# Key-value products of a linear attention: head pairs on 64-lane halves, or single heads on 64x64 quarters of the array

## The chip, the cores and the metric

The kernel runs on one core of a Trainium2 chip. The metric is the device time of one execution in microseconds (us), the median of several runs. A hardware profile of one execution is shown beside it: PE is TensorE's matmuls, PEld its weight loads, DVE is VectorE, ACT is ScalarE, POOL is GpSimd and SP is SyncE, whose queue issues most DMAs. L295 is line 295 of the kernel file.

## What is computed

Inputs are q, k and v of shape 8 batches x 8 heads x 576 positions x 64 (f32), and two weight matrices, 512 x 2048 and 2048 x 512 (f32). The output is 4608 x 512 in f32.

```python
def _attn_ref(q, k, v):
    q_s = np.exp(q - np.max(q, axis=-1, keepdims=True))
    q_s = q_s / (np.sum(q_s, axis=-1, keepdims=True) + 1e-09)
    k_s = np.exp(k - np.max(k, axis=2, keepdims=True))
    k_s = k_s / (np.sum(k_s, axis=2, keepdims=True) + 1e-09)
    kv = np.einsum('bhsd,bhse->bhde', k_s, v)
    return np.einsum('bhsd,bhde->bhse', q_s, kv)

x = attn_out.transpose(0, 2, 1, 3).reshape(8 * 576, 8 * 64)
h = x @ w_in
out = np.maximum(0.01 * h, h) @ w_out
```

The part that matters here is `kv`: for each batch and head, a 64 x 64 matrix, summed over 576 positions, of exponentiated k against v. The division by the sum over positions is done on the result: the sum of each k column comes out of the same product if v has a further column of ones.

## The kernel before

**Layout.** One batch of q, k or v lies in SBUF as 128 partitions x 4 x 9 x 64. Eight heads are spread so: partitions 0 to 63 hold the first head of each of four pairs and partitions 64 to 127 the second (index `hh` is 0 or 1), 64 partitions are 64 groups of positions, and r runs over the 9 positions of a group. In the program's names, head 2 x hl + hh has its rows in half hh and its place hl among four; hl is written as 2 x gg + hp.

**Attention of one batch.** k's maximum over positions (DVE, and for batch 0 PE), the subtraction (POOL or DVE), the exponential into `ke` in bf16 (ACT, L203), a cast of v into `vb` in bf16 (`v_cast`, ACT or POOL). q goes through its own maximum, exponential, sum and normalisation into `qe`, and is transposed (by PE for batches 0 and 1, by DMA for the others). Then three steps follow on the array:

1. `kv` (batches 1 to 7, L295) or `kv_pair` (batch 0, in two halves, L371): the key-value products. The stationary operand is `ke` of one row half (64 partitions) and of two heads (hp 0 and 1), 64 x 128; the moving operand is `vb` of the same 64 partitions, 129 columns: 64 of one head, 64 of the other and one column of ones. The result, 128 x 129 in PSUM, has the two wanted 64 x 64 products on its diagonal, two unwanted ones beside them, and the sums in column 128. Nine matmuls (r) accumulate into one result. The two row halves alternate in program order and write to two PSUM banks. One batch takes 2 x 9 x 2 = 36 matmuls.
2. `kd_make` (L310, L313), for batch 0 `kd_rec` and `kd_one` (L382, L387): DVE takes the reciprocal of the sums and writes the diagonal blocks, scaled, into `kd`, whose other blocks are zero. `kd_one` does it with one instruction over 128 x 128 and a mask `block` of ones on the diagonal blocks.
3. `attend` (L418) or `attend_x` (L446): `kd`, 128 x 128, times the transposed q, 256 to 320 columns at a time, and a copy to `xT` by ACT or DVE.

**Two dense layers.** The 4608 rows of x are taken in 9 tiles of 512. For each, `layer1` (L458) makes 16 blocks of hidden units by 4 matmuls each of 512 columns, `leaky` (L467, ACT) writes them to `gj` in bf16, and `layer2` (L479) adds 16 matmuls for each of 4 groups of 128 rows; the result is copied (L473, mostly DVE) and stored. The first tile is worked in two halves of 256 columns.

**Order.** The schedule is written out by hand. `at(t, u, ...)` hangs attention steps of a batch onto step u of dense tile t, and `run(t, u)` calls them there, so on PE's queue a batch's key-value stage stands between two matmuls of the dense layers, some 4 us or more before the first `attend` of that batch. PE works its queue in order. Batch 0 has no dense work ahead of it: its stages run in the first 20 us, padded by `wake`, matmuls on zeros (L324), while the weights of the layers are still being loaded by POOL's queue (L133).

The PSUM results `pkv` come from a pool of six one-bank buffers which the layers share.

Of the kernel before, what the change touches and what calls it, by code (L numbers as in the profile page):

```python
# [8 lines left out]
FP32 = mybir.dt.float32  # L9
BF16 = mybir.dt.bfloat16  # L10
AF = mybir.ActivationFunctionType
ALU = mybir.AluOpType
# [7 lines left out]
L = 64  # L20
R = 9
# [4 lines left out]
def kernel(  # L26
# [9 lines left out]
    nc = tc.nc  # L36
# [3 lines left out]
    B, H, S, D = q.shape  # L40
# [6 lines left out]
    P = 128  # L47
# [7 lines left out]
    const_pool = ctx.enter_context(tc.tile_pool(name="const", bufs=1))  # L55
# [11 lines left out]
    psB_pool = ctx.enter_context(tc.tile_pool(name="psB", bufs=6, space=bass.MemoryType.PSUM))  # L67
    psO_pool = ctx.enter_context(tc.tile_pool(name="psO", bufs=2, space=bass.MemoryType.PSUM))
    BANK_TAG = "bank2k"


    def load(src, b, name, cuts):
# [15 lines left out]
    st = [{} for _ in range(B)]  # L88
# [7 lines left out]
        out=st[0]["q"][:, :, RB].rearrange("p h r d -> p h (r d)"),  # L96
        in_=qflat[:, :, RB].rearrange("p h r d -> p h (r d)"),
# [8 lines left out]
    block = const_pool.tile([P, P], FP32)  # L106
# [9 lines left out]
    xT = xT_pool.tile([P, NB, T], BF16)  # L116


    vb2 = [const_pool.tile([P, R, 2, 130], BF16, name=f"vb{i}") for i in range(2)]
    kd2 = [const_pool.tile([P, NB, P], BF16, name=f"kd{i}") for i in range(2)]  # L120
    for i in range(2):
        nc.gpsimd.memset(vb2[i][:, :, :, 128:129], 1.0)
        nc.gpsimd.memset(kd2[i], 0.0)


# [81 lines left out]
        )  # L207

    def v_cast(eng, b, gg):
        o = vb2[b % 2][:, :, gg, 0:128].rearrange("p r (h d) -> p h r d", h=2)  # L210
        i = st[b]["v"][:, 2 * gg : 2 * gg + 2]
        if eng is nc.scalar:
            eng.copy(out=o, in_=i)
        else:
            eng.tensor_copy(out=o, in_=i)  # L215
# [69 lines left out]
        )  # L285


    def kv(b):

        pkv = [psB_pool.tile([P, 2, 130], FP32, name="pkv", tag=BANK_TAG) for _ in range(2)]  # L290
        for gg in range(2):
            for r in range(R):
                for hh in range(2):
                    rows = slice(hh * L, (hh + 1) * L)
                    nc.tensor.matmul(  # L295
                        pkv[hh][:, gg, 0:129],
                        lhsT=st[b]["ke"][rows, r, 2 * gg : 2 * gg + 2].rearrange(
                            "p h d -> p (h d)"
                        ),
                        rhs=vb2[b % 2][rows, r, gg, 0:129],  # L300
                        start=(r == 0),
                        stop=(r == R - 1),
                    )
        st[b]["pkv"] = pkv

    def kd_make(b):
        for hh in range(2):
            pkv = st[b]["pkv"][hh]
            krec = small_pool.tile([P, 2, 1], FP32, name="krec")
            nc.vector.reciprocal(out=krec, in_=pkv[:, :, 128:129])  # L310
            for hp in range(2):
                p0 = hp * D
                nc.vector.tensor_tensor(  # L313
                    out=kd2[b % 2][p0 : p0 + D, 2 * hh : 2 * hh + 2, p0 : p0 + D],
                    in0=pkv[p0 : p0 + D, :, p0 : p0 + D],
                    in1=krec[p0 : p0 + D].to_broadcast([D, 2, D]),
                    op=ALU.mult,
                )
# [45 lines left out]
        )  # L364

    def kv_pair(b, gg):
        pkv = [psB_pool.tile([P, 130], FP32, name="pkv1", tag=BANK_TAG) for _ in range(2)]
        for r in range(R):
            for hh in range(2):
                rows = slice(hh * L, (hh + 1) * L)  # L370
                nc.tensor.matmul(  # L371
                    pkv[hh][:, 0:129],
                    lhsT=st[b]["ke"][rows, r, 2 * gg : 2 * gg + 2].rearrange("p h d -> p (h d)"),
                    rhs=vb2[b % 2][rows, r, gg, 0:129],
                    start=(r == 0),
                    stop=(r == R - 1),
                )
        st[b]["pkv", gg] = pkv

    def kd_rec(b, gg, hh):  # L380
        st[b]["krec", gg, hh] = krec = small_pool.tile([P, 1], FP32, name="krec1")
        nc.vector.reciprocal(out=krec, in_=st[b]["pkv", gg][hh][:, 128:129])  # L382

    def kd_one(eng, b, gg, hh):
        pkv, krec = st[b]["pkv", gg][hh], st[b]["krec", gg, hh]
        o = kd2[b % 2][:, 2 * hh + gg]
        eng.scalar_tensor_tensor(  # L387
            out=o, in0=pkv[:, 0:P], scalar=krec, in1=block, op0=ALU.mult, op1=ALU.mult
        )

    def q_transpose(b, r0, n):
# [145 lines left out]
    k_sub_ps(0, 0, HB)  # L537
    k_exp(0, slice(1, 2))
    v_cast(nc.scalar, 0, 0)
    v_cast(nc.scalar, 0, 1)  # L540
    k_sub_ps(0, 1)
    nc.gpsimd.tensor_copy(out=gate[:, 0:1], in_=st[0]["k"][:, HL - 1, R - 1, D - 1 : D])  # L542
    load_w_in(1)
    k_exp(0, H1)
    q_first_rec(0, RA)
    q_norm(0, RA)
    kv_pair(0, 0)
    wake(4)
    q_transpose(0, 0, 4)
    kv_pair(0, 1)  # L550
    for hh in range(2):
        kd_rec(0, 0, hh)
        kd_one(nc.vector, 0, 0, hh)
    q_keep(nc.scalar, 0, 0, 4, slice(0, 4, 2))
    q_keep(nc.vector, 0, 0, 4, slice(1, 4, 2))
    attend(0, [0, 2], 0, 256, nc.scalar)
    wake(3)
    kd_rec(0, 1, 0)
    kd_rec(0, 1, 1)
    kd_one(nc.vector, 0, 1, 0)  # L560
    kd_one(nc.vector, 0, 1, 1)
    q_max(0, R1)
    q_sub(nc.gpsimd, 0, R1)
# [25 lines left out]
    at(0, 15, lambda: q_max(1, RB), lambda: q_sub(nc.gpsimd, 1, RB))  # L589
    at(0, 29, lambda: k_exp(1, H1))  # L590
    at(0, 31, lambda: v_cast(nc.scalar, 1, 0), lambda: k_exp(1, H0))
    at(0, 33, lambda: q_exp(1, RA), lambda: q_sum(1, RA), lambda: q_norm(1, RA))
    at(0, 33, lambda: v_cast(nc.scalar, 1, 1), lambda: q_exp(1, RB), lambda: q_sum(1, RB))
    at(0, 41, lambda: kv(1))
    at(0, 41, lambda: q_norm(1, RB), lambda: kd_make(1))
    for r0 in (0, 2):
        at(0, 41, lambda r0=r0: q_transpose(1, r0, 2), lambda r0=r0: q_keep(nc.scalar, 1, r0, 2))
# [10 lines left out]
    def plan(b, o):  # L608
        t = b - 2
        at(t, o, lambda: k_begin(b), lambda: q_begin(b), lambda: k_tree(b, ALLH))  # L610
        at(t, o + 3, lambda: k_allmax(b), lambda: k_sub(nc.gpsimd, b, ALLH))
        at(t, o + 7, lambda: q_max(b, ALLR), lambda: q_sub(nc.gpsimd, b, ALLR))
        at(t, o + 11, lambda: k_exp(b, ALLH))
        at(t, o + 12, lambda: v_cast(nc.gpsimd, b, 0), lambda: v_cast(nc.gpsimd, b, 1))
        at(t, o + 16, lambda: q_exp(b, ALLR))
        at(t, o + 18, lambda: q_sum(b, ALLR))
        at(t, o + 21, lambda: q_norm(b, ALLR))
        kvu, pu = o + (24 if b == 3 else 25), o + (33 if b == 3 else 34)
        at(t, kvu, lambda: kv(b))
        at(t, kvu + 1, lambda: kd_make(b))  # L620
        at(t, o + 22, lambda: q_turn(b))
        for i in range(8):
            at(t, pu + i // 2, lambda i=i: attend_x(b, i // 2, XR[i % 2], nc.scalar))


    def plan2():
        b = 2
        at(1, 0, lambda: k_begin(b), lambda: q_begin(b), lambda: k_tree(b, ALLH))
        at(1, 3, lambda: k_allmax(b))
        at(1, 6, lambda: k_sub(nc.vector, b, H0), lambda: k_sub(nc.vector, b, H1))  # L630
        at(1, 9, lambda: k_exp(b, ALLH))
        for rs in XR:
            at(1, 9, lambda rs=rs: q_max(b, rs), lambda rs=rs: q_sub(nc.gpsimd, b, rs))
        at(1, 13, lambda: v_cast(nc.gpsimd, b, 0), lambda: v_cast(nc.gpsimd, b, 1))
        for i, rs in enumerate(XR):
            at(1, (13, 16)[i], lambda rs=rs: q_exp(b, rs), lambda rs=rs: q_sum(b, rs), lambda rs=rs: q_norm(b, rs))
            at(1, (15, 17)[i], lambda rs=rs: q_turn(b, rs))
        at(1, 23, lambda: kv(b))
        at(1, 24, lambda: kd_make(b))
        for i in range(8):  # L640
            at(1, 28 + i // 2, lambda i=i: attend_x(b, GS[i % 4], XR[i // 4], nc.scalar))
# [91 lines left out]
```

## Time and profile before

| | us |
|---|---|
| median of 3 runs | 293.1 (292.87 to 293.29) |
| the profiled execution, whole | 293.27 |
| its span, first to last instruction | 291.5 |
| TensorE busy (of the span) | 280.2 (96%) |
| ScalarE busy | 149.7 (51%) |
| VectorE busy | 147.0 (50%) |
| GpSimd busy | 85.5 (29%) |
| granted TensorE clock, mean | 1.000 |

Busy time of PE is the union of its matmuls' records; a matmul's record is its latency, and records of neighbouring matmuls overlap, so a group's busy time is less than its count times its mean. The chain that ended last is the sequence of work, followed back from the last instruction, in which each piece was released by the one before it. Times in a timeline or chain are counted from the start of the span.

### The profile page before, as it was taken

How to read it: one execution, taken by the hardware profiler on the slowest of the kernel's cores; microseconds unless marked ns; L12 is line 12 of the kernel's file. 1: busy time of each engine (PE TensorE's matmuls, PEld its weight loads, DVE VectorE, ACT ScalarE, POOL GpSimd, SP SyncE). 2: the span in 40 equal slices, each digit the busy share in tenths (PEclk: the TensorE clock that was granted, in tenths of full speed). 3: DMA queues.
4: the chain of work that ended last, by engine and by line, in shares of the span. 5: the costliest groups of instructions: out<-in, count | busy, mean ns of one | idle time of the engine just before them, and what ended most of it. 6: DMA issues, size and time to landing. Idle time of an engine off the chain costs nothing.

```text
span 291.5 us, 4277 instructions
## 1 busy us (share of the span) xinstructions
PE 280.2 (96%) x1645; PEld 139.9 (48%) x1672; DVE 147.0 (50%) x244; ACT 149.7 (51%) x268; POOL 85.5 (29%) x61
## 2 busy tenths in 40 slices
PE   8697999999999999999999999999999999999995
PEld 3265845444544544454444544554455444444443
DVE  2947957896790796289276546645541200110011
ACT  4957683568168506941684339533953066017400
POOL 4545280008039208703910391029200000000000
PEclk9999999999999999999999999999999999999999
DMA  7999999597639454973299139913141310131032
GB/s 255 314 202 378 256 176 397 139 286 270 124 89 338 162 119 108 336 211 86 65 338 250 36 72 318 287 36 74 36 81 38 72 36 1 38 75 33 0 73 73
DMA packets 36580, 45.76 MB, mean 157 GB/s; under 512 B 15952, under 2 KB 19280, under 8 KB 36560
## 3 DMA queue, kind: packets, MB, share of 16 engines
q1 hardware_dynamic: 33120, 41.16, 48.4%
q0 software_dynamic: 3280, 4.20, 8.3%
q8 instruction: 13, 0.21, 0.3%
q10 hardware_dynamic: 160, 0.13, 0.1%
q14 instruction: 7, 0.06, 0.1%
HBM read 36.70 MB, written 9.44 MB: 158 GB/s over the span
## 4 chain that ended last, share of the span: by engine, by line
PE 89%; DMA 3%; DVE 1%; issue 1%; ACT 1%; POOL 1%; ACTq 0%
PE pout L479 43%; PE ph L458 41%; DMA w_in_sb<-in_moe_w_in_dram 3%; PE pkv L295 3%; PE po L446 2%; DVE k_raw L362 1%; PE psum_qt L395 1%; POOL w_in_sb L133 0%; ACT gj L467 0%; ACT xT L428 0%; PE po L418 0%; DVE out_sb L473 0%; POOL gate L542 0%; ACTq L467 0%
## 5 line engine op out<-in xcount | busy, mean ns | idle before, releaser
L479 PE MATMUL pout<-w_out_sb,gj 128*128 128x512 bf16 (+2 forms) x580 | 129.6, 373 | 0.6
L458 PE MATMUL ph<-xT,w_in_sb 128*128 128x512 bf16 (+1 forms) x626 | 126.8, 357 | 3.4 <-ACT xT L428 1.4
L467 ACT ACTIVATE gj<-ph 128x512 bf16<-128x512 f32 x144 | 82.5, 603 | 58.1 <-PE ph L458 57.5
L458 PEld LDWEIGHTS <-w_in_sb 128*128 128x128 bf16 x640 | 62.1, 98 | 64.8 <-issue 4.1
L479 PEld LDWEIGHTS <-gj 128*128 128x128 bf16 x592 | 57.0, 98 | 62.1 <-ACT gj L467 0.4
L473 DVE COPY out_sb<-pout 128x512 f32<-128x512 f32 (+1 forms) x34 | 22.7, 675 | 86.2 <-PE pout L479 80.7
L195 POOL TENSOR_TENSOR k_raw<-k_raw,kall 128x2304 f32<-128x2304 f32 (+1 forms) x6 | 29.1, 4846 | 83.5 <-DVE kall L187 56.3
L273 DVE TENSOR_REDUCE qsum<-qe 128x36 f32<-128x2304 bf16 (+4 forms) x11 | 19.8, 1799 | 37.4 <-ACT qe L264 37.4
L256 POOL TENSOR_TENSOR q_raw<-q_raw,qmax 128x2304 f32<-128x2304 f32 (+4 forms) x11 | 31.1, 2839 | 25.4 <-DVE qmax L226 25.4
L452 ACT CAST xT<-po 128x320 bf16<-128x320 f32 (+1 forms) x48 | 16.8, 402 | 41.2 <-PE po L446 41.2
L203 ACT ACTIVATE ke<-k_raw 128x2304 bf16<-128x2304 f32 (+2 forms) x11 | 17.6, 1596 | 10.3 <-POOL k_raw L195 8.6
L280 DVE TENSOR_TENSOR qe<-qe,qrec 128x2304 bf16<-128x2304 bf16 (+4 forms) x12 | 21.7, 1811 | 0.4
L226 DVE TENSOR_REDUCE qmax<-q_raw 128x36 f32<-128x2304 f32 (+4 forms) x11 | 19.4, 1789 | 0.0
L264 ACT ACTIVATE qe<-q_raw 128x2304 bf16<-128x2304 f32 (+4 forms) x11 | 16.9, 1533 | 0.8 <-POOL q_raw L256 0.8
L215 POOL CAST vb<-v_raw 128x1152 bf16<-128x1152 f32 x12 | 13.5, 1153 | 0.0
L324 PE MATMUL pout<-zero 128*128 128x512 bf16 x29 | 9.6, 470 | 1.5 <-POOL zero L101 1.3
L162 DVE TENSOR_TENSOR t<-k_raw 128x1024 f32<-128x1024 f32 (+1 forms) x10 | 10.1, 1011 | 0.5 <-DMA k_raw<-in_k_dram 0.2
L162 DVE TENSOR_TENSOR t<-t 128x256 f32<-128x256 f32 (+2 forms) x20 | 9.6, 478 | 0.7
L446 PE MATMUL po<-qX,kd 128*128 128x320 bf16 (+1 forms) x48 | 9.8, 286 | 0.0
L473 ACT COPY out_sb<-pout 128x512 f32<-128x512 f32 (+1 forms) x3 | 1.7, 563 | 14.9 <-PE pout L479 14.9
L295 PEld LDWEIGHTS <-ke 64*128 64x128 bf16 x252 | 7.2, 93 | 3.0 <-ACT gj L467 1.7
L313 DVE TENSOR_TENSOR kd<-pkv,krec 64x128 bf16<-64x128 f32 x28 | 8.1, 289 | 0.7
(57 smaller groups left out, 104.8 us busy)
## 6 DMA issues: line engine op xcount, KB each, us to landing
out_dram<-out_sb SPq DMA_DIRECT2D x70, 128.0 KB, 2.4
q_raw<-in_q_dram SPq DMA_DIRECT2D x7, 1152.0 KB, 8.4
v_raw<-in_v_dram SPq DMA_DIRECT2D x7, 1152.0 KB, 11.4
k_raw<-in_k_dram SPq DMA_DIRECT2D x6, 1152.0 KB, 6.1
k_raw<-in_k_dram SPq DMA_DIRECT2D x4, 576.0 KB, 5.7
w_in_sb<-in_moe_w_in_dram POOLq DMA_DIRECT2D x8, 256.0 KB, 6.7
w_out_sb<-in_moe_w_out_dram POOLq DMA_DIRECT2D x3, 512.0 KB, 13.2
v_raw<-in_v_dram SPq DMA_DIRECT2D x2, 576.0 KB, 7.7
```

The lines of the kernel that those rows point to most:

```text
L162: nc.vector.tensor_tensor(out=o, in0=i0, in1=i1, op=ALU.max)
L195: eng.tensor_tensor(out=ks, in0=ks, in1=st[b]["kall"][:, hs].unsqueeze(2).to_broadcast([P, n, R, D]), op=ALU.subtract,)
L203: nc.scalar.activation(out=st[b]["ke"][:, :, hs].rearrange("p r h d -> p h r d"), in_=st[b]["k"][:, hs], func=AF.Exp,)
L226: nc.vector.tensor_reduce(out=m, in_=st[b]["q"][:, :, rs], axis=AX.X, op=ALU.max)
L256: eng.tensor_tensor(out=qs, in0=qs, in1=st[b]["qmax", rs.start].unsqueeze(3).to_broadcast([P, HL, n, D]), op=ALU.subtract,)
L264: nc.scalar.activation(out=st[b]["qe"][:, rs].rearrange("p r h d -> p h r d"), in_=st[b]["q"][:, :, rs], func=AF.Exp,)
L273: nc.vector.reduce_sum(out=qsum, in_=st[b]["qe"][:, rs], axis=AX.X)
L280: nc.vector.tensor_tensor(out=qes, in0=qes, in1=st[b]["qrec", rs.start].unsqueeze(3).to_broadcast([P, n, HL, D]), op=ALU.mult,)
L458: nc.tensor.matmul(ph, lhsT=w_in_sb[:, cb, j * P : (j + 1) * P], rhs=xT[:, cb, c0 : c0 + n], start=(i == 0 and first), stop=(i == NB - 1 a ...
L467: nc.scalar.activation(out=o, in_=ph, func=AF.Prelu, alpha=LEAKY_SLOPE)
L473: copy(out=out_sb, in_=pout)
L479: nc.tensor.matmul(pout, lhsT=g_sb[j // 2][:, j % 2, tsub * P : (tsub + 1) * P], rhs=w_out_sb[:, j, os], start=(j == 0), stop=(j == NF - 1),)
```

## The change

The products are made for each head alone. The stationary operand is 64 x 64 (one head, one row half), the moving operand 65 columns (that head's v and a column of ones of its own), and the result goes to partitions 0 to 63 or 64 to 127 of the same PSUM buffer by the head's place hp. Four matmuls, one for each (hp, hh), now stand where two stood, 72 per batch. `vb` holds two blocks of 66 columns for each pair in place of one of 130, and the reciprocal and the kd steps read columns 0 to 63 and 64 of the narrower result. In `kd_one` the 64 columns are read twice by a broadcast, and the mask keeps the diagonal blocks.

```diff
-    vb2 = [const_pool.tile([P, R, 2, 130], BF16, name=f"vb{i}") for i in range(2)]
+    vb2 = [const_pool.tile([P, R, 2, 2, D + 2], BF16, name=f"vb{i}") for i in range(2)]
...
-        nc.gpsimd.memset(vb2[i][:, :, :, 128:129], 1.0)
+        nc.gpsimd.memset(vb2[i][:, :, :, :, D : D + 1], 1.0)
...
-        o = vb2[b % 2][:, :, gg, 0:128].rearrange("p r (h d) -> p h r d", h=2)
+        o = vb2[b % 2][:, :, gg, :, 0:D].rearrange("p r h d -> p h r d")
...
-    def kv(b):
-
-        pkv = [psB_pool.tile([P, 2, 130], FP32, name="pkv", tag=BANK_TAG) for _ in range(2)]
-        for gg in range(2):
-            for r in range(R):
+    def kv_quads(b, gg, outs):
+        for r in range(R):
+            for hp in range(2):
                 for hh in range(2):
                     rows = slice(hh * L, (hh + 1) * L)
                     nc.tensor.matmul(
-                        pkv[hh][:, gg, 0:129],
-                        lhsT=st[b]["ke"][rows, r, 2 * gg : 2 * gg + 2].rearrange(
-                            "p h d -> p (h d)"
-                        ),
-                        rhs=vb2[b % 2][rows, r, gg, 0:129],
+                        outs[hh][hp * D : (hp + 1) * D, 0 : D + 1],
+                        lhsT=st[b]["ke"][rows, r, 2 * gg + hp],
+                        rhs=vb2[b % 2][rows, r, gg, hp, 0 : D + 1],
                         start=(r == 0),
                         stop=(r == R - 1),
                     )
+
+    def kv(b):
+
+        pkv = [psB_pool.tile([P, 2, D + 2], FP32, name="pkv", tag=BANK_TAG) for _ in range(2)]
+        for gg in range(2):
+            kv_quads(b, gg, [pkv[hh][:, gg] for hh in range(2)])
...
-            nc.vector.reciprocal(out=krec, in_=pkv[:, :, 128:129])
+            nc.vector.reciprocal(out=krec, in_=pkv[:, :, D : D + 1])
...
-                    in0=pkv[p0 : p0 + D, :, p0 : p0 + D],
+                    in0=pkv[p0 : p0 + D, :, 0:D],
...
     def kv_pair(b, gg):
-        pkv = [psB_pool.tile([P, 130], FP32, name="pkv1", tag=BANK_TAG) for _ in range(2)]
...
+        pkv = [psB_pool.tile([P, D + 2], FP32, name="pkv1", tag=BANK_TAG) for _ in range(2)]
+        kv_quads(b, gg, pkv)
...
-        nc.vector.reciprocal(out=krec, in_=st[b]["pkv", gg][hh][:, 128:129])
+        nc.vector.reciprocal(out=krec, in_=st[b]["pkv", gg][hh][:, D : D + 1])
...
-            out=o, in0=pkv[:, 0:P], scalar=krec, in1=block, op0=ALU.mult, op1=ALU.mult
+            out=kd2[b % 2][:, 2 * hh + gg].rearrange("p (h d) -> p h d", h=2),
+            in0=pkv[:, 0:D].unsqueeze(1).to_broadcast([P, 2, D]),
+            scalar=krec,
+            in1=block.rearrange("p (h d) -> p h d", h=2),
+            op0=ALU.mult,
+            op1=ALU.mult,
```

More of the change, by code (lines that the diff above doesn't have):

```diff
@@ L366, in kv_pair @@
     def kv_pair(b, gg):
-        pkv = [psB_pool.tile([P, 130], FP32, name="pkv1", tag=BANK_TAG) for _ in range(2)]
[L368 to L377, printed above, removed]
+        pkv = [psB_pool.tile([P, D + 2], FP32, name="pkv1", tag=BANK_TAG) for _ in range(2)]
+        kv_quads(b, gg, pkv)
         st[b]["pkv", gg] = pkv
@@ L381, in kd_rec @@
         st[b]["krec", gg, hh] = krec = small_pool.tile([P, 1], FP32, name="krec1")
-        nc.vector.reciprocal(out=krec, in_=st[b]["pkv", gg][hh][:, 128:129])
+        nc.vector.reciprocal(out=krec, in_=st[b]["pkv", gg][hh][:, D : D + 1])
     def kd_one(eng, b, gg, hh):
         pkv, krec = st[b]["pkv", gg][hh], st[b]["krec", gg, hh]
-        o = kd2[b % 2][:, 2 * hh + gg]
         eng.scalar_tensor_tensor(
-            out=o, in0=pkv[:, 0:P], scalar=krec, in1=block, op0=ALU.mult, op1=ALU.mult
+            out=kd2[b % 2][:, 2 * hh + gg].rearrange("p (h d) -> p h d", h=2),
[4 more added lines that the diff above has]
+            op1=ALU.mult,
         )
```

## The prediction

> **What bounds the kernel now.** I read the page's first two parts, then the chain that ended last, then the groups kept apart by shape, then the timeline around one key-value stage.
>
> ```profile
> PE 280.2 (96%) x1645; PEld 139.9 (48%) x1672; DVE 147.0 (50%) x244; ACT 149.7 (51%) x268; POOL 85.5 (29%) x61
> ...
> PE 89%; DMA 3%; DVE 1%; issue 1%; ACT 1%; POOL 1%; ACTq 0%
> ```
>
> TensorE is busy from end to end and holds 89% of the chain. The chain in order of time shows where the key-value products (L295) stand in it, and where those of batch 0 (L371) do not:
>
> ```profile
> 14.94 8.36 DMA w_in_sb<-in_moe_w_in_dram
> 23.31 0.14 issue
> 23.44 1.69 PE ph L458 x14
> ...
> 44.78 1.13 PE pkv L295 x36
> ...
> 67.27 7.00 PE pout L479 x32
> 74.26 1.13 PE pkv L295 x36
> 75.39 0.32 PE pout L479
> ...
> 79.81 0.27 PE po L446 x2
> ```
>
> For batches 1 to 7 the same piece, 36 matmuls in 1.13 us, stands seven times on the chain with TensorE's own work directly before and after it: what a stage saves or costs moves the end by as much. Batch 0's two half stages run at 13.5 and 15.7 us, while the chain is a weight transfer that ends at 23.31; TensorE idles 1.15 us at 23.44 for it. Seven stages count, not eight.
>
> The groups by shape give the prices:
>
> ```profile
> L458 PE MATMUL ph<-xT,w_in_sb 128*128 128x256 bf16 x128 | 15.1, 272 | 2.6 <-ACT xT L428 1.4 <-DMA w_in_sb<-in_moe_w_in_dram 1.2
> L295 PE MATMUL pkv<-vb,ke 64*128 64x129 bf16 x252 | 8.4, 216 | 0.0
> L313 DVE TENSOR_TENSOR kd<-pkv,krec 64x128 bf16<-64x128 f32 x28 | 8.1, 289 | 0.7
> L330 PE MATMUL pout<-identf,nmax 128*4 128x128 f32 x8 | 1.0, 273 | 0.0
> ```
>
> 252 matmuls are seven stages of 36. The 216 ns is latency; what counts is the distance from one start to the next.
>
> **The change: pace of a matmul.** From the chain, 56 matmuls of 256 columns take 6.11 us (at 30.03), 109 ns each, and 49 recorded ones of 512 columns in 10.74 us are 50 at 215 ns (matmul records can be missing). The difference, 106 ns for 256 columns, is 0.414 ns a column, with 3 ns left over. So 129 columns take 56.4 ns and 65 columns 29.9 ns. The timeline of a stage proves the first and a row of 64 columns the second:
>
> ```profile
> 74.20 1.20 PE L295 MATMUL pkv<-vb,ke 64*128 64x129 bf16 x36
> 75.32 0.82 PE L479 MATMUL pout<-w_out_sb,gj 128*128 128x512 bf16 x2
> ```
>
> ```profile
> 29.75 0.28 PE L418 MATMUL po<-qT,kd 128*128 128x64 bf16 x4
> 29.86 0.49 PE L458 MATMUL ph<-xT,w_in_sb 128*128 128x256 bf16 x3
> ```
>
> From the first start to the next layer's is 1.12 us. 36 matmuls at 56.4 would be 2.03; 17 steps of 56.4 are 0.96, and 0.16 is left for the last one to drain before the full array starts. So the two row halves already run side by side, a pair for the price of one. The 64-column row gives 0.11/4 = 28 ns.
>
> **What is removed and added.** A stage loses 36 matmuls of 64x128 weights on 129 columns and gets 72 of 64x64 on 65: from 18 pairs to 18 steps of four (two row halves, two column halves). TensorE issues 36 more weight loads and 36 more matmuls per stage, 288 of each in all.
>
> If four run side by side, 18 steps go from 56.4 to 29.9: 18 x 26.5 = 0.477 us saved per stage. That column halves do so is shown by the kernel's one use of them, the broadcast of the maxima (L351):
>
> ```profile
> 9.27 0.20 PEld L351 LDWEIGHTS kallp<-identf,kr 128*64 128x64 f32 x4 [0.77 <-DVE kr L346]
> 9.27 0.44 PE L351 MATMUL kallp<-identf,kr 128*64 128x128 f32 x4 [0.39 <-DVE kr L346]
> ```
>
> Two halves, two f32 passes each. The L330 row has eight such passes of 128 f32 columns on one place of the array in 1.04 us, which is 7 distances of 109 ns and a last one of 273. Four in a row would take 3 x 109 + 273 = 600 ns; two beside two take 109 + 273 = 382 and the first weight load. Measured 440. They overlap, and the second loads (all four begin within 0.20 - 0.13 = 0.07 us) lie beside the first matmuls.
>
> **The weight load** is the unknown. The full-array loads of L458 last 98 ns by record, f32 loads of 4 columns (L330) 87, of 64 columns (L351) 132 to 135. Taking 83 to 87 as fixed, 64 f32 columns cost up to 49 ns. No row loads 64 bf16 columns. Lower bound: half of what a 128-column load costs above the fixed part (98 - 83 to 98 - 87, so 11 to 15), about 7. Upper bound: the 49 of f32. A moving f32 column costs twice a bf16 one (109 against 56 ns at 128), so I take half of 49, 25 ns, hidden under the 29.9 of the matmuls before; at 49 it sets the pace. A stage's first load has no cover: 25 instead of 12, 0.013 us lost (0.037 at the upper end).
>
> By the Trainium skill, TensorE: Matmul & The Clock Gate, sections "Weight-path perf modes" and "LDWEIGHTS", the fast load needs 128 columns and a plain one takes P/1.2 ns: 53 ns for 64, as an estimate. By that the stage would save 18 x 3.4 - 41 = 20 ns, 0.1 us in all: no change. The f32 row's 49 is near it, and no row here shows it for bf16.
>
> **Edges.** Before the stage TensorE drains: the timeline has the last two pout matmuls from 73.67 for 0.59 us, so with 0.38 for one by record the last began at 73.88, 0.32 before the stage where 0.215 is its own pace; on leaving, 0.16 remains. Both changes of array shape stay, one in and one out. The last four drain 64 columns earlier, but I count nothing for it.
>
> **Beside the path, at nothing.** The casts of v (POOL and ScalarE) write the same 64-element runs with another stride; POOL is 29% busy. VectorE's reciprocals and kd products read as many elements (the L313 row's 64x128, and 128x128 in batch 0); kd is first used at 79.81, 4.4 us after the stage, so even twice their 289 ns each would hide. The column of ones grows from 18 to 36 elements in two setup instructions. No DMA of the kernel changes, no wait is added; four writers fill two banks where two did. ScalarE (51%) and VectorE (50%) wait for TensorE, so an earlier stage is taken up. Batch 0's saving is hidden behind the weight transfer; its loss would be too, up to the 1.15 us.
>
> **Sum.** (0.477 - 0.013) x 7 = 3.25 us. The profiled execution took 293.27 us, its span 291.5 and 1.77 around it: 293.27 - 3.25 = 290.0. The median of the three runs is 293.1, 0.17 lower; by it, 289.85. I say 290.0. With a step of 40 ns in place of 29.9, a load a little too long to hide, the gain is 18 x 16.4 x 7 = 2.1 us, so this case's own range is 289.4 to 291.3.
>
> **Rivals.** *TensorE's instruction stream becomes the bound (slower).* Four matmuls and four loads must come every 29.9 ns. The fastest stream in the trace is one load and one matmul in 28 to 31 ns (36 in 1.12, four in 0.11). If that is how fast they are issued and not how fast the array takes them, 72 pairs cost 72 x 28 = 2.02 us against 1.01: +1.0 a stage, +7.0, 300.3. Instructions can stand ready: L295's queued semaphore wait is passed at 40.7 and its matmuls start at 44.7, so about 4.0/0.216 = 19 pairs were ahead. With 19 of 72 ready, 53 x 28 = 1.48: +0.47 a stage, +3.3, 296.6. It decides from 14 ns a pair upward (56.4/4). For it: no row is faster for longer. Against it: the four loads of L351 within 0.07 us, and that the 28 ns of 64 columns is explained by the columns alone.
>
> The Trainium skill, TensorE: Matmul & The Clock Gate, section "Wait — 56ns, not 53.3ns?", has a floor of about 25 ns from start to start, however few the columns. If that held for all quarters together, an estimate is 72 x 25 = 1.80 against 1.01, +5.5 us, 298.8. On average no stretch here goes below it, so the trace does not contradict it.
>
> *The weight load sets the pace (no change).* At 49 ns a step, plus 2 to swap, 18 x 5.4 - 37 = 60 ns a stage, 0.4 us: 292.9. At 56 it is a loss of about 0.2. For it speaks the f32 row, the nearest of the same width.
>
> *The column halves exclude each other:* two steps of 29.9 for one of 56.4, 18 x 3.4 x 7 = +0.4, 293.7. The L351 row speaks against it.
>
> **Chances.** A measurement of this kernel can tell about 0.2%, 0.6 us. Four side by side with a hidden load: 0.52. Load-bound or halves in turn, both within 0.6: 0.13. Issue-bound: 0.35, most of it below 297 because some instructions stand ready and the true pace may lie between 14 and 28 ns. Cases of both signs hold most of the chance, so the range goes from 289.4 to 297.0 and leaves out the hardest third of the issue case and a little below.
>
> **What would show it.** L295's line in the changed kernel should have 504 matmuls of 64*64 and 64x65, and the chain seven pieces of about 0.67 us in place of 1.13. Loads recorded at about 110 ns speak for the hidden load, at 130 for the load-bound case. A piece of 1.5 us or more, with loads and matmuls evenly 14 ns apart, is the issue-bound case. The prediction is wrong if the pieces do not shrink, or if they shrink and the idle time turns up before ph or gj.

## The result, and the profile after

The changed kernel takes 290.49 us in the median of nine runs (289.99 to 292.28) against 293.17 us before (292.87 to 293.45): a ratio of 0.9924, 95% interval 0.9899 to 0.995. The profiled execution took 290.49 us, 2.78 less than the one of before, its span 288.7 us, 2.8 less. Three of the nine runs, near 292.25, had a mean granted TensorE clock of 0.994; the others are between 289.99 and 290.74. The faster ones are what the kernel does at full clock; the lowered clock is taken up below.

The page's first part and its chain by engine, for the changed kernel:

```profile
PE 278.3 (96%) x1960; PEld 137.4 (48%) x1960; DVE 146.9 (51%) x244; ACT 149.5 (52%) x268; POOL 85.5 (30%) x61
...
PE 85%; DMA 10%; POOL 2%; issue 1%; SPq 1%; ACT 0%; DVE 0%; POOLq 0%
```

More instructions on TensorE, less time on it, and the three other engines as they were. (All quarter matmuls stand on one line, L293, since a helper makes them for all batches; the layers moved to L455 and L476.) In the chain in order of time (start us, us, what) a key-value stage is now:

```profile
13.03 6.82 DMA w_in_sb<-in_moe_w_in_dram
...
26.78 12.70 DMA w_out_sb<-in_moe_w_out_dram
39.48 0.04 issue
39.52 5.34 PE pout L476 x24
44.86 0.73 PE pkv L293 x72
...
73.94 0.73 PE pkv L293 x72
74.68 4.42 PE pout L476 x20
...
180.64 0.71 PE pkv L293 x72
```

Five stages fell from 1.13 to 0.73 us and two to 0.71: 5 x 0.40 + 2 x 0.42 = 2.84 us, the whole of the difference. Nothing came of batch 0: the first stage that counts begins at 44.86 us, where it began at 44.78. Up to 39.5 us the chain of this execution runs through the weight transfers, the second of which (w_out) had not been on it; in two later profiles of the same kernel it is not on it, and the first stage begins at 44.67 and 44.45 us. The same stage in the timeline, and the rows of its loads and matmuls by shape:

```profile
73.56 0.38 PE L476 MATMUL pout<-w_out_sb,gj 128*128 128x512 bf16 x1
73.87 0.80 PE L293 MATMUL pkv<-vb,ke 64*64 64x65 bf16 x72
74.61 0.39 PE L476 MATMUL pout<-w_out_sb,gj 128*128 128x512 bf16 x1
```

```profile
L455 PE MATMUL ph<-xT,w_in_sb 128*128 128x256 bf16 x128 | 15.1, 272 | 3.0 <-DMA w_in_sb<-in_moe_w_in_dram 1.6 <-ACT xT L425 1.4
L293 PE MATMUL pkv<-vb,ke 64*64 64x65 bf16 x576 | 6.5, 194 | 1.0 <-ACT vb L213 0.8 <-ACT ke L203 0.2
L293 PEld LDWEIGHTS <-ke 64*64 64x64 bf16 x576 | 5.5, 106 | 4.7 <-ACT gj L464 1.7 <-ACT vb L213 1.3 <-issue 1.3
```

0.74 us from the first start to the next layer's, 1.12 before. 72 matmuls of 29.9 ns in a row would take 2.15 us; four run side by side. In the trace the first four matmuls of a stage start within 10 ns of one another. The second set of four starts 53 ns after the first, the sixteen sets behind it 32 ns apart on average (32.1 in five stages, 31.6 and 31.8 in two). The first row has the other half of batch 0's story: the wait for the second half of w_in grew from 1.2 to 1.6 us, about by what batch 0 was sooner (the matmuls behind its second half start at 15.95 us, and started at 16.31 in the kernel before); it scatters, with 2.0 and 1.8 us in the two later profiles.

### The profile page after: what moved, and what is told of

It is laid out like the page before. It is cut to its first block, busy times and chain, and to the rows that moved or that the text cites. A ratio compares the mean times of both kernels' runs of the same rounds, so it can differ in the third digit from the quotient of the medians.

```text
span 288.7 us, 4880 instructions
## 1 busy us (share of the span) xinstructions
PE 278.3 (96%) x1960; PEld 137.4 (48%) x1960; DVE 146.9 (51%) x244; ACT 149.5 (52%) x268; POOL 85.5 (30%) x61
## 4 chain that ended last, share of the span: by engine, by line
PE 85%; DMA 10%; POOL 2%; issue 1%; SPq 1%; ACT 0%; DVE 0%; POOLq 0%
PE pout L476 42%; PE ph L455 38%; DMA w_out_sb<-in_moe_w_out_dram 4%; DMA k_raw<-in_k_dram 4%; DMA w_in_sb<-in_moe_w_in_dram 2%; PE po L443 2%; PE pkv L293 2%; POOL w_in_sb L133 1%; POOL w_out_sb L140 1%; PE psum_qt L392 0%; SPq L79 0%; PE po L415 0%; SPq L508 0%; ACT xT L425 0%; DVE out_sb L470 0%
## 5 line engine op out<-in xcount | busy, mean ns | idle before, releaser
L476 PE MATMUL pout<-w_out_sb,gj 128*128 128x512 bf16 (+2 forms) x592 | 130.5, 373 | 0.1
L455 PE MATMUL ph<-xT,w_in_sb 128*128 128x512 bf16 (+1 forms) x640 | 127.5, 358 | 3.1 <-DMA w_in_sb<-in_moe_w_in_dram 1.6
L455 PEld LDWEIGHTS <-w_in_sb 128*128 128x128 bf16 x640 | 62.1, 98 | 65.0 <-issue 4.6
L476 PEld LDWEIGHTS <-gj 128*128 128x128 bf16 x592 | 57.0, 98 | 62.3 <-issue 0.4
L293 PEld LDWEIGHTS <-ke 64*64 64x64 bf16 x576 | 5.5, 106 | 4.7 <-ACT gj L464 1.7
```

Source lines behind the costliest of these rows:

```text
L455: nc.tensor.matmul(ph, lhsT=w_in_sb[:, cb, j * P : (j + 1) * P], rhs=xT[:, cb, c0 : c0 + n], start=(i == 0 and first), stop=(i == NB - 1 a ...
L476: nc.tensor.matmul(pout, lhsT=g_sb[j // 2][:, j % 2, tsub * P : (tsub + 1) * P], rhs=w_out_sb[:, j, os], start=(j == 0), stop=(j == NF - 1),)
```

## The experiments

All are edits of the changed kernel. Times at the side are those of the kernel before on the same chip.

**Column halves further apart.** What makes the gain: four side by side, or narrower matmuls and smaller weights?

```diff
-        for r in range(R):
-            for hp in range(2):
+        for hp in range(2):
+            for r in range(R):
```

> The changed kernel with the loop over the two column halves outside the loop over r: the same 72 matmuls of 64x64 on 65 columns, but neighbours in the queue now sit on the same column half, so at most two (the row halves) can run side by side. If the gain comes from four running side by side, a stage is 36 steps of about 30 ns, 1.08 us plus the drain, 0.5 us longer than in the changed kernel (592 ns from first to last start): 7 x 0.5 = 3.5 us, 294.0 us, no better than before. If it comes from narrower matmuls and smaller weights as such, the time stays at 290.5.

Measured 291.91 us against 293.14, ratio 0.9956 (0.9943 to 0.997): half of the gain is lost. Its chain and timeline:

```profile
73.75 0.97 PE pkv L293 x67
74.72 4.42 PE pout L476 x20
```

```profile
73.68 1.04 PE L293 MATMUL pkv<-vb,ke 64*64 64x65 bf16 x72
74.66 0.39 PE L476 MATMUL pout<-w_out_sb,gj 128*128 128x512 bf16 x1
```

The same matmuls in another order cost 0.24 us more a stage, 7 x 0.24 = 1.7 us. That is about the time lost: 291.91 is 1.4 us above the changed kernel's 290.49 and 1.8 above the 290.09 of its version with pairs in batch 0, run on the same chip (below). So it is the overlap of the column halves that pays. But the loss is half of what was expected: 854 ns from first to last start, not 1.1 us. In the trace the second column half's first matmul (known by a record of 214 ns, like that of a stage's first) starts at 73.87, while the last three steps of the first half, ahead of it in the program, still start at 73.89 to 73.96. The same happens at each of the three changes of half in a stage, so 9 of the 36 steps lie beside others, and the 27 left, at 32 ns, are 0.86 us: the overlap that remains explains the stage without any gain from narrower matmuls. Matmuls on different quarters are thus not bound to the order of the program, though it was said ahead of the prediction that PE works its queue in order. That was tested by itself:

```diff
+        order = [(r0 + i, hp) for r0 in range(0, R, 3) for hp in range(2) for i in range(3)]
+        for r, hp in order:
```

> The changed kernel with the column halves alternating after every three r in place of every one: three steps on the one half, then three on the other. In the kernel with the column halves in two runs of nine, the second half began while the last three steps of the first were still queued, 854 ns in all against 36 x 31.6 = 1138 for steps strictly in turn: as if each quarter kept some three matmuls waiting of its own. If so, blocks of three overlap almost fully: stages near 0.6 to 0.65 us from first to last start, 290.1 to 290.7. If matmuls start strictly in the order of the program, only the ends of blocks overlap: some 24 of 36 distances remain, 0.8 us or more, 291.5 and above.

Measured 290.28 us against 293.1, ratio 0.9901 (0.9887 to 0.9915), as fast as the changed kernel. In the timeline the stage takes 0.78 us to the next layer, 0.05 more than with halves alternating each step:

```profile
73.31 0.85 PE L293 MATMUL pkv<-vb,ke 64*64 64x65 bf16 x72
74.09 0.39 PE L476 MATMUL pout<-w_out_sb,gj 128*128 128x512 bf16 x1
```

Blocks of three overlap almost wholly, 655 ns from first to last start, and the second half's first matmul starts 20 ns into the stage, ahead of the first half's second step at 52: steps strictly in order cannot do that. It fits some three matmuls waiting for each quarter by themselves; how they wait is not shown.

**What sets the 32 ns of a step.** The columns, the weight load, or the instruction stream?

```diff
+        for r in range(R): ...       # the same loops over hp and hh
+                        outs[hh][hp * D : (hp + 1) * D, 0:9],
+                        lhsT=st[b]["ke"][rows, r, 2 * gg + hp],
+                        rhs=vb2[b % 2][rows, r, gg, hp, 0:9],
         for r in range(R): ...       # as it was, 65 columns
```

> The changed kernel with each group of 36 matmuls run twice into the same place: first on 9 columns only (overwritten at once), then on all 65. With 9 columns the array has almost nothing to do. If only the array sets the pace, the 9-column sets of four take the time of a 64-column weight load or less (about 21 ns), and the 65-column sets stay at 31 to 32 ns. If the instruction stream is a limit just below the surface, at the 8.3 ns for a load and a matmul that the last loads of a stage show, sets of four take 33 ns once the instructions that stood ready (about 32 pairs) are used up, whatever their columns. A stage then has 144 pairs: (144 - 32) x 8.3 = 0.93 us plus some 0.3 us, about 1.2 us from first to last start against 0.59.

One execution, 297.3 us against 293.14. In its chain, L293 is the pass on 9 columns and L304 the one on 65:

```profile
101.26 0.38 PE pkv L293 x36
101.65 0.31 PE pkv L304 x35
101.95 0.30 PE pkv L293 x35
102.26 0.32 PE pkv L304 x36
```

The pieces of 36 take 0.30 us with 9 columns and 0.31 to 0.32 with 65. The columns do not set the pace. First to last start is 1195 ns for 144 pairs, 8.4 ns for a load and a matmul, which is the 1.2 us expected of the instruction stream. But the total does not prove the stream: in both passes on 9 columns, the first of which has instructions standing ready, the sets are 31 to 32 ns apart (but for the last one or two of the second pass), where the expectation had 21 for the array and 33 for the stream. Only the last eight distances of a stage, on 65 columns, are 33 to 34 ns, with a load beginning every 8.3 ns.

What parts the two is the kernel with the column halves further apart. The last steps of its stages stand on one column half alone, two matmuls each, so that a step needs half the instructions, and they too are 32 ns apart (224 ns for seven). So the 32 ns belong to a quarter, to a load and a matmul on it, and neither to the columns nor to the stream. An estimate from the records gives the load about 21 of them (a stage's first matmul is recorded at 214 ns, later ones mostly at 193); what the rest is, no run shows. Right behind lies the second limit, 33 ns for eight instructions. That this one is the instruction stream is argued from the even 8.3 ns between loads, not shown.

The time itself is explained by 7 x (1.195 + 0.126 - 0.736) = 4.1 us for the longer stages and by two waits of 1.15 us, such as no other profile here has. One lies in a stage, the other among the layers (at 158.2 us):

```profile
185.71 0.41 PE L304 MATMUL pkv<-vb,ke 64*64 64x65 bf16 x27
187.28 0.28 PE L304 MATMUL pkv<-vb,ke 64*64 64x65 bf16 x9 [1.15 <-issue]
```

290.5 + 4.1 + 2.3 = 296.9, 0.4 short of the 297.3 measured.

**Which batches pay.** Quarters in seven batches, pairs in batch 0, and the reverse. The pairs read `vb` in its new layout, 2 x 65 columns:

```diff
+    def kv_halves(b, gg, outs): ...
+                    outs[hh],
+                    lhsT=st[b]["ke"][rows, r, 2 * gg : 2 * gg + 2].rearrange("p h d -> p (h d)"),
+                    rhs=vb2[b % 2][rows, r, gg, :, 0 : D + 1],
```

> The changed kernel, but batch 0 keeps head pairs on row halves (64x128 weights on 130 columns); batches 1 to 7 use quarters. If batch 0 is hidden behind the weight transfer, the time is that of the changed kernel at full clock, 290.0 to 290.7. If batch 0 counted, it would lose 2 x 0.2 us: 290.9. In three of the changed kernel's nine runs the mean granted clock was 0.994 and the time 1.75 us longer, in none of the kernel before. If TensorE's longer idle time in the first 24 us (1.57 against 1.15 us at 23.5) is the cause, no run here has it; if it is the quarters as such, about a third of the runs have it.

> The other half: quarters in batch 0 only, head pairs on row halves (130 columns) in batches 1 to 7. If only the seven later stages count: 293.1 to 293.3, as before (130 for 129 columns is 18 x 0.4 ns a stage, 0.05 us in all). If batch 0 brought part of the gain, 292.7 or less. If the idle time early in the kernel is what lowers the clock, about a third of the runs show 0.994 and 294.9.

With pairs in batch 0: 290.09 us (290.05 to 290.2) against 293.14, ratio 0.9896 (0.9881 to 0.9911). With quarters in batch 0 only: 292.92 us, ratio 0.9995 (0.9986 to 1.0003), not told from no change; its seven stages on the chain are as before:

```profile
74.77 1.14 PE pkv L305 x36
75.92 4.42 PE pout L488 x20
```

So seven stages pay and batch 0 does not: with pairs in batch 0 the first stage on the chain begins at 44.36 us, against 44.45 to 44.86 in three profiles of the changed kernel. Repeated beside the unaltered changed kernel:

> Quarters in batches 1 to 7, head pairs in batch 0, again. By the theory that batch 0 is hidden, 290.0 to 290.7 at full clock, no different from the changed kernel beside it. If the shorter batch 0 has to do with the lowered clock, none of these runs has it and the two differ in how far they scatter; if not, this one has it as often.

> The changed kernel unaltered, beside the next run on one chip. 290.0 to 290.9 at full clock; of its fifteen runs so far four had a mean granted clock of 0.994 and 292.0 to 292.3, so one or two of the runs here.

290.55 us (290.07 to 291.11) and 290.09 us (289.86 to 290.22), both against 293.24. The lead of the version with pairs in batch 0 has turned round; no version run here is shown to be faster than the changed kernel.

**The lowered clock.** Is it TensorE's longer idle time near 23.5 us?

> The changed kernel unaltered, on the chip of the runs beside it, for the granted clock. 290.0 to 290.7 at full clock. If TensorE's idle time before 23.5 us is what lowers the clock, about a third of the runs show 0.994 and 292.25; if it belonged to that one chip or hour, none does.

```diff
+            if half == 0 and j == 8:
+                wake(5)
```

> The changed kernel with five more matmuls on zeros (1.08 us) in front of the first-layer work that waits for the second half of the weights near 23.5 us, where TensorE idles 1.57 us. They fit into the wait, so they cost nothing: 290.0 to 290.7. If the idle time is what lowers the clock, no run shows 0.994; if not, as many as the changed kernel beside it.

The changed kernel took 290.36 us against 293.1 (ratio 0.9911, 0.9892 to 0.993), with one run of six at 0.994 and 291.97. With five more matmuls on zeros it took 290.58 us (ratio 0.9914, 0.99 to 0.9928), none of six runs at 0.994. The gap was filled, and another wait took part of its place, as the groups of that kernel show:

```profile
L476 PE MATMUL pout<-w_out_sb,gj 128*128 128x512 bf16 (+2 forms) x580 | 129.7, 373 | 1.2 <-DMA w_out_sb<-in_moe_w_out_dram 0.5
L455 PE MATMUL ph<-xT,w_in_sb 128*128 128x512 bf16 (+1 forms) x626 | 127.0, 357 | 2.5 <-ACT xT L425 1.4 <-DMA w_in_sb<-in_moe_w_in_dram 0.3
```

The counts do not settle the cause. The changed kernel shows 0.994 in 4 of 19 runs, its version with pairs in batch 0 in none of 8, but the one with quarters in batch 0 only in none of 11, and that one has the same work up to 44 us. Nor do the 8 runs of the two other loop orders show it, with quarters in all batches. Profiled executions were all near 1.0, so where in the kernel the clock falls was not seen. It stays open. What it costs is read from the runs: 0.006 of 290 us, 1.7 us, in a fifth of them.

## Why the prediction was right, point by point

*Seven stages count:* right. Their savings on the chain sum to 2.84 us, and the version with quarters in batch 0 alone gains nothing. The named cover, the wait for w_in, grew by 0.4 us.

*Four side by side:* right, by the order of the loops. The reason given, that L351's two column halves overlap, carried over to matmuls with their own weights.

*The step of 29.9 ns:* near the 32 measured, but for a wrong reason, and so by luck. The working took it from the 65 columns, with the load hidden under them; the run on 9 columns has the same step, where the working would have given 25 ns, its load. The pace belongs to the quarters: a load and a matmul on one take 32 ns, whatever the columns. That is nearer to the rival in which the weight load sets the pace, only that the rival priced the step at 51 ns and what was measured is 32. (Its loss of 0.2 us at 56 ns leaves out the 2 ns to swap, which no run shows; with them it would be 0.5.)

*The size of a stage's gain:* 464 ns predicted; from the first start to the next layer's it is 1128 before and 736 in five stages, 710 in two, so 392 and 418 were gained. The loss of 13 ns for the first load came as predicted. Sixteen steps gave 396 (404 in the two), not 424, since a step is 32 and not 29.9. The larger part is the end of a stage: 18 x 26.5 counts a gain for the last step as well, but from the last set's first start to the next layer it is 169 ns now (150 in the two) against 150 before. Nothing was gained there: the 64 columns less to drain, which the prediction meant to leave out and which that last 26.5 stands for, did not show. In all 0.45 us of the 3.25 did not come.

*The weight load:* 25 ns was worked out, half of the f32 row's 49. The records make it about 21, an estimate as said above. Records of 102 to 111 ns are those named for the hidden load, but the sign misled: the step does not shorten when the columns do. By the Trainium skill's P/1.2 (TensorE: Matmul & The Clock Gate, "LDWEIGHTS") it would have been 53 ns and the gain 0.1 us; here the measurement decides against it, with 32 ns for the whole step.

*The rest of the sum,* the edges: in five of the stages the loads of the last four matmuls come behind a gap of 34 ns, and the matmuls have records of 212 ns (195 in the other two), so their load is not hidden. That is the difference between 0.73 and 0.71, and it had no term.

*The instruction stream:* the rival was priced at 28 ns a pair and decides from 14; it is 8.3 at most. With 33 ns for four pairs it lies beside the quarters' own 32 and hardly above it. The floor of 25 ns from start to start that the Trainium skill gives (TensorE: Matmul & The Clock Gate, "Wait — 56ns, not 53.3ns?") does not hold across quarters: 72 starts in 592 ns are 8.3 ns apart.

*The size:* 290.0 predicted, 290.49 median, 290.1 to 290.4 on the other chips; the 0.45 us above are the difference. What the range held upward for, the slower stream, did not come. The lowered clock in some runs was not foreseen either, but the median run is at full clock.

## What to carry to other kernels

Where half of a matmul's output is thrown away and the contraction has only 64 rows, single products on quarters of the array can take the place of pairs, at some 32 ns for four with 65 columns; 9 columns took as long, so fewer columns win nothing. Alternate the column halves in program order at least every three steps: runs of nine cost more than half of the gain. Count a gain only for the stages that stand on the chain: the same edit in the batch that runs while weights arrive was worth nothing.

## What the runs showed of the hardware that was not expected

Matmuls on different column halves start out of program order, by about three steps. The 9-column pass takes as long as the 65-column one. And in the kernel with 144 load and matmul pairs a stage TensorE twice stood still for 1.15 us with nothing to wait for in the profile, until 159.4 and 187.3 us. Its instruction transfers grew:

```profile
q8 instruction: 20, 0.33, 0.5%
```

against 15 packets in the changed kernel. That these waits are for instructions is not shown, and the trace hardly speaks for it: no transfer of that queue runs during them. The last ones before began at 156.94 and 184.96 us and took 0.93 and 0.96, so they had ended 0.35 and 0.2 us before TensorE stopped. The cause stays open.
